# One way for h - tanh h instead of two: an expert kernel on one core, with a new order of its token stage

## Chip, core and metric

The kernel runs on one core of one Trainium2 chip. The metric is the device time in microseconds (us) of a run, as the median of several runs; lower is better. Everything is float32; large products split an operand into a rounded part and its remainder and use three matmuls.

## What is computed

Three layers, one behind the other (inputs are drawn at random; here cut to what matters):

```
X = rfft(x, axis=1)                       # x: 8 x 3072 x 256
Yr = Xr @ w_r - Xi @ w_i + b_r            # Yi alike; both shrunk by 0.01 towards 0
y = irfft(Y)                              # 24576 tokens x 256 from here on
h = y @ w_in                              # 2048 wide
x2 = (h - tanh(h)) @ w_out                # 256 wide
logits = x2 @ phi                         # 32 slots
d = softmax(logits, axis=0)               # over the 24576 tokens
slot_out = experts(d.T @ x2)              # 8 experts of 4 slots: relu(s @ w1[e]) @ w2[e]
out = softmax(logits, axis=1) @ slot_out
```

## The kernel before

The program has three stages. `spectral_phase` makes y by transforms in two factors, in 96 steps (8 batches of 12), and stores it in DRAM. Beside them it takes 32 pieces of the weights w_in and w_out through `load_w`, `narrow`, `use_w` and `fold_w`: a piece of w_in is split for the hidden layer (L457, L458), stored to `wi32`, turned by two transposes (L465) and multiplied into `wy` (L477); a piece of w_out is turned and multiplied with phi into `wp` (L487, L488). So `wp` is -w_out phi, and `wy` is w_in w_out phi.

`token_phase` works on 48 chunks of 512 tokens. h stands there with its 2048 rows in eight pairs of 128 (p = 0 to 7, four pairs of pairs w = 0 to 3). Chunk 0 is multiplied plainly (`plain`); from chunk 1 on `wino` uses a Winograd form: per w seven products P 1 to 7 of six matmuls each (L768), in three of six PSUM banks. ScalarE evicts P 1, 6, 7 and 4 into g (L779), VectorE adds what is in the other two banks (A, L786), ScalarE puts tanh over each finished g tile (G, L790, 1024 columns). So g holds tanh h. The logits take g with `wp` (L911) and, for the term in h, y itself with `wy` (L919, y loaded again by `load_raw`). For the dispatch d.T @ (h - tanh h), g is turned by VectorE's 32 x 32 transposes (T, L860), regrouped by DMAs from SBUF to SBUF (`reg`, L876) and multiplied with the turned softmax (D, L1042); y is turned too (L849), regrouped with g and multiplied (DY, L828), summed in `accy` (L836), and after the last chunk multiplied with w_in from `wi32` (L1213) and subtracted. The softmax over slots is divided here, in `combine_end` (L1019 to L1025), and stored in DRAM as `ctd`. For the tokens' own split into a rounded part and a remainder GpSimd subtracts (L666, L675, L681).

The order within a chunk is written out by hand: `PLAN` lists steps (name, which chunk relative to the present one, arguments), and `chunk(c)` issues them in that order. Every engine executes its own instructions in the order in which they were issued; so a step that waits holds up what stands behind it on its engine.

In the last chunk and after it, weights of the experts are loaded into tiles that come free (`weights`, `ew.load`, L1347, L1349, all from SyncE's queue), the last chunk is turned on TensorE (`turn_pe`, L889), and `expert_phase` multiplies slots, experts and, in 24 pairs of chunks, the output, which ScalarE and VectorE evict in halves (L1441, L1442).

```
            g = gs[c, p] if u else g_tile(c, p)
            nc.scalar.activation(g[:, u], o, AF.Tanh)
...
            nc.scalar.activation(wp[:, r, :], pw, AF.Copy, scale=-1.0)
...
            for name, d, *args in PLAN:
                k = c + d
```

## Time and profile before

| | |
|---|---|
| Median of 3 runs | 2144.37 us (2140.1 to 2145.66) |
| Profiled execution, first to last instruction (span) | 2137.1 us |
| Mean granted TensorE clock | 0.980 of full speed |
| TensorE matmuls busy | 2052.8 us, 96% of the span |
| VectorE busy | 1849.2 us, 87% |
| ScalarE busy | 1396.0 us, 65% |
| GpSimd busy | 642.6 us, 30% |
| Moved by DMA | 499.68 MB, 234 GB/s |

The profile is of one execution, and the only time that it has of its own is the span from its first to its last instruction; the median of the runs is 7.3 us longer, which is what lies around that span. In the profile PE is TensorE's matmuls, PEld its weight loads, DVE is VectorE, ACT ScalarE, POOL GpSimd, SP SyncE; SPq and ACTq are the DMA queues of SyncE and ScalarE. A matmul of float32 counts as two instructions, one of a rounded operand as one. A duration is that of one instruction from its start to its end; neighbours on TensorE overlap, so what one costs in a row is the distance of starts. "idle before" names what ended an engine's wait.

### The profile page before, as it was taken

To read this page: it belongs to the slowest core of one execution; us is meant where nothing else is said; L and a number is where in the kernel's file an instruction comes from. 1 tells how busy PE (TensorE), PEld (TensorE's weight loads), DVE (VectorE), ACT (ScalarE), POOL (GpSimd) and SP (SyncE) were. 2 spreads that over 40 slices of the span, in tenths; PEclk is the share of its full clock that TensorE was granted. 3 is DMA by queue.
4 is the path that set the end of the run, shared out by engine and by line. 5 is a ranking of instruction groups with operands and counts; after the bars stand their busy time and mean duration, and the time that the engine had idled before them with its cause. 6 is when DMAs were issued, how large, how long until landed. Compare 5 with 4: busy or idle time off the path is not lost.

```text
span 2137.1 us, 54258 instructions
## 1 busy us (share of the span) xinstructions
PE 2052.8 (96%) x21302; PEld 1732.6 (81%) x21302; DVE 1849.2 (87%) x3587; ACT 1396.0 (65%) x2309; POOL 642.6 (30%) x655
## 2 busy tenths in 40 slices
PE   5899999999999999999999999999999999999985
PEld 2678888887887888888888888888888888888743
DVE  3999888999995899999999999999999999999624
ACT  2456666666566777777777777777777777777614
POOL 0444444444443422222222222222222222222000
PEclk7999999999999999999999999999999999999986
DMA  9788999899657788888888888888888888888899
GB/s 273 225 242 267 284 283 286 269 283 293 202 198 205 194 208 213 207 213 209 207 203 209 208 208 210 219 204 208 209 206 208 209 206 210 214 209 208 254 401 388
DMA packets 260927, 499.68 MB, mean 234 GB/s; under 512 B 37312, under 2 KB 147648, under 8 KB 260416
## 3 DMA queue, kind: packets, MB, share of 16 engines
q1 hardware_dynamic: 259632, 494.60, 84.8%
q8 instruction: 169, 2.77, 0.6%
q10 hardware_dynamic: 1040, 1.61, 0.2%
q14 instruction: 86, 0.70, 0.1%
HBM read 166.28 MB, written 108.00 MB: 128 GB/s over the span
## 4 chain that ended last, share of the span: by engine, by line
PE 82%; DVE 8%; DMA 5%; ACT 2%; issue 1%; SPq 1%; POOL 0%; ACTq 0%; DVEq 0%; POOLq 0%
PE ph L768 44%; PE pl L911 8%; PE pd L1042 8%; PE pmix L328 4%; PE pi L413 4%; PE pf L287 3%; PE pi L385 3%; PE pa L328 3%; PE pf L251 2%; DVE sw L378 2%; DMA ewt<-in_moe_w 1%; DVE t L369 1%; DVE xml L299 1%; PE pl L828 1%; PE pl L919 1%
## 5 line engine op out<-in xcount | busy, mean ns | idle before, releaser
L779 ACT ACTIVATE g<-ph 128x512 f32<-128x512 f32 x752 | 448.6, 597 | 323.9 <-PE ph L768 285.8
L768 PE MATMUL ph<-th,s 128*128 128x256 f32 x2256 | 499.4, 288 | 3.3 <-ACT g L779 3.2
L860 DVE STREAM_TRANSPOSE gt<-g 128x512 f32<-128x512 f32 x752 | 472.0, 679 | 4.7 <-ACT g L742 4.0
L786 DVE TENSOR_TENSOR g<-ph,g 128x512 f32<-128x512 f32 x564 | 367.4, 672 | 85.3 <-ACT g L779 79.9
L790 ACT ACTIVATE g<-g 128x1024 f32<-128x1024 f32 x376 | 380.7, 1050 | 46.4 <-DVE g L786 46.4
L768 PEld LDWEIGHTS ph<-th,s 128*128 128x128 f32 x2256 | 383.7, 189 | 32.1 <-issue 19.4
L681 POOL TENSOR_TENSOR tl<-tr,th 128x512 fp32r<-128x512 f32 x94 | 121.5, 1293 | 949.4 <-ACT th L680 949.4
L768 PE MATMUL ph<-tl,s 128*128 128x256 f32 x1128 | 318.1, 282 | 0.0
L768 PE MATMUL ph<-yh,wl 128*128 128x256 f32 x1128 | 316.0, 280 | 0.0
L768 PE MATMUL ph<-y,wh 128*128 128x256 f32 x1128 | 315.4, 280 | 0.0
L768 PE MATMUL ph<-yh,wh 128*128 128x256 f32 x1128 | 315.1, 279 | 0.0
L378 POOL TENSOR_TENSOR sw<-t,c 64x256 f32<-64x256 f32 x192 | 169.7, 884 | 169.8 <-DVE c L370 130.9
L768 PEld LDWEIGHTS ph<-tl,s 128*128 128x128 f32 x1128 | 213.5, 189 | 0.0
L768 PEld LDWEIGHTS ph<-yh,wh 128*128 128x128 f32 x1128 | 213.0, 189 | 0.0
L768 PEld LDWEIGHTS ph<-y,wh 128*128 128x128 f32 x1128 | 212.3, 188 | 0.0
L768 PEld LDWEIGHTS ph<-yh,wl 128*128 128x128 f32 x1128 | 212.2, 188 | 0.0
L911 PE MATMUL pl<-g,wp 128*32 128x256 f32 x3072 | 193.2, 381 | 0.0
L1042 PE MATMUL pd<-gq,et 128*32 128x256 f32 x3008 | 172.7, 381 | 3.3 <-DMA gq<-gt 3.3
L1042 PEld LDWEIGHTS pd<-gq,et 128*32 128x32 f32 x3008 | 99.0, 111 | 68.1 <-issue 3.7
L287 PEld LDWEIGHTS pf<-f,a 128*128 128x128 f32 x768 | 102.0, 194 | 54.6 <-issue 37.8
L911 PEld LDWEIGHTS pl<-g,wp 128*32 128x32 f32 x3072 | 91.2, 110 | 56.4 <-issue 0.7
L413 PE MATMUL pi<-i,v 96*128 96x128 f32 x1024 | 134.5, 275 | 1.0 <-ACT yt L424 0.6
(216 smaller groups left out, 4279.4 us busy)
## 6 DMA issues: line engine op xcount, KB each, us to landing
gq<-gt SPq DMA_DIRECT2D x752, 160.0 KB, 3.5
gq<-gt SPq DMA_DIRECT2D x752, 128.0 KB, 3.2
xt<-in_x SPq DMA_DIRECT2D x64, 448.0 KB, 5.5
vd<-vs SPq DMA_DIRECT2D x96, 256.0 KB, 3.4
v<-vd SPq DMA_DIRECT2D x64, 384.0 KB, 5.3
yd<-yt SPq DMA_DIRECT2D x48, 512.0 KB, 5.7
y<-yd SPq DMA_DIRECT2D x48, 512.0 KB, 3.4
yr<-yd SPq DMA_DIRECT2D x48, 512.0 KB, 4.7
```

The lines of the kernel that those rows point to most:

```text
L287: nc.tensor.matmul(p[:, :, h, gg, :], t[:, gg, 128 * h:128 * h + 128], f2[:, 128 * g:128 * g + 128], start=True, stop=True,)
L328: nc.tensor.matmul(o, st[u], w[m], start=first and k == 0, stop=last and k == 2)
L378: eng.tensor_tensor(out=v[64 * ri:64 * ri + 64, gg], in0=t[q, e], in1=c[q, e], op=ALU.subtract)
L413: nc.tensor.matmul(p[:, a, :], t[:, 4 * u + a, :], i2[:, 96 * n2:96 * n2 + 128], start=True, stop=True)
L681: nc.gpsimd.tensor_tensor(out=lo, in0=t, in1=hi.bitcast(F32), op=ALU.subtract)
L768: nc.tensor.matmul(o[:, 256 * j:256 * j + 256], a[u][:, 128 * j:128 * j + 128], y[v], start=new and j == 0 and k == 0, stop=n in (2, 3, 4) ...
L779: nc.scalar.activation(e[n], o.rearrange("p (j n) -> p j n", j=2), AF.Copy)
L786: nc.vector.tensor_tensor(out=h, in0=o, in1=h, op=ALU.add)
L790: nc.scalar.activation(g, g, AF.Tanh)
L860: nc.vector.transpose(out=t[:, :, :, 2 * (p % 4) + u, :], in_=g[:, u, :].rearrange("p (q k i) -> p q k i", q=4, k=4))
L911: nc.tensor.matmul(lp[c][q:q + 32, 0:256], wp[:, 2 * p + f, :], half_of(c, gs[c, p + f // 2][:, f % 2], h), start=p == 0 and f < 2, stop=F ...
L1042: nc.tensor.matmul(o[32 * a:32 * a + 32, f], ex[c][:, k, :], g[a][:, k], start=k == 0, stop=k == 3)
```

## The change

g now holds h - tanh h itself. A finished quarter of two g tiles (512 columns, `quarter`) goes through tanh into one of four buffers `t0` to `t3` (G, `gate`), and GpSimd subtracts that from g (U, `ungate`); for P 4 the tanh is read from PSUM into g, without the eviction of before, and VectorE subtracts it from PSUM. All ways through y go: `load_raw`, `turn_yr`, `dy_mm`, `accum_y`, the logits with `wy`, the fold of w_in and `wi32`, and the product with w_in at the end; `wp` is now +w_out phi. The order is a new PLAN with U as a step. The division of the combine weights moves behind the output's matmuls, as a scale of its eviction in four pieces (`zt`); the sums are kept in `zs`. Output tiles lie in two PSUM tiles of half the size. In the last chunk each unit of G and U is issued as it gets ready, T and `reg` of the chunk before as soon as they can be, and eight loads (`early`) are issued from ScalarE's queue at set points.

```
-    ("G", -1, 6), ("P", 0, 0, 6), ("A", 0, 0, 2), ("T", -1, 7), ("loady", 1), ("splity", 1), ("L", -1, 0), ("DY", -2), ("L", -1, 2),
...
+    ("U", -1, 3, 3), ("U", -1, 3, 2), ("L", -1, 2), ("A", 0, 0, 2), ("U", -1, 3, 7), ("G", -1, 2, 3), ("D", -2), ("G", 0, 0, 2),
...
@@ use_w, fold_w
-                nc.sync.dma_start(out=wi32[128 * r:128 * r + 128, 256 * q:256 * q + 256], in_=t)
...
-            else:
-                nc.sync.dma_start(out=wo32.rearrange("(p F) m -> p F m", F=16)[:, r], in_=t)
+                return
+            nc.sync.dma_start(out=wo32.rearrange("(p F) m -> p F m", F=16)[:, r], in_=t)
...
+            if src is w_in:
+                return
...
-                    nc.tensor.matmul(pw, wt[:, k, :], wp[:, 2 * q + k, :], start=k == 0, stop=k == 1)
...
-            nc.scalar.activation(wp[:, r, :], pw, AF.Copy, scale=-1.0)
+            nc.scalar.activation(wp[:, r, :], pw, AF.Copy)
@@ token_phase
-        homes = chain(["g5"] + [f"g{k}" for k in range(5)], cycle([f"g{k}" for k in range(5)] + [f"x{k}" for k in range(4)] + ["x5"]))
+        homes = chain(
+            ("g5", "g0", "g1", "g2", "g3", "g4", "g0", "g1"),
+            cycle(("g2", "g5", "x0", "x2", "x3", "x5", "x1", "g0", "g1", "g3", "g4")),
+        )
...
             nc.scalar.activation(g[:, u], o, AF.Tanh)
+            nc.vector.tensor_tensor(out=g[:, u], in0=o, in1=g[:, u], op=ALU.subtract)
...
-            e = {1: ha and ha[:, :, 0:256], 6: ha and ha[:, :, 256:512], 7: hb and hb[:, :, 256:512], 4: hb and hb[:, :, 0:256]}
+            e = {1: ha and ha[:, :, 0:256], 6: ha and ha[:, :, 256:512], 7: hb and hb[:, :, 256:512]}
...
-        def gate(c, p):
-            g = gs[c, p]
-            nc.scalar.activation(g, g, AF.Tanh)
...
+        def gate(c, w, n):
+
+            g, o = quarter(c, w, n)
+            if n == 4:
+                nc.scalar.activation(g, o, AF.Tanh)
             else:
+                t = th[c, w, n] = ew.tyq.tile([128, 2, 256], F32, tag=f"t{next(units) % 4}", name="tanh")
+                nc.scalar.activation(t, g, AF.Tanh)
+
+        def ungate(c, w, n):
+
+            g, o = quarter(c, w, n)
+            if n == 4:
+                nc.vector.tensor_tensor(out=g, in0=o, in1=g, op=ALU.subtract)
             else:
+                eng = nc.vector if c == nch - 1 and sum(left) < 2 else nc.gpsimd
+                eng.tensor_tensor(out=g, in0=g, in1=th.pop((c, w, n)), op=ALU.subtract)
...
-            if p == 6:
-                for kk in range(2):
-                    for h in range(2):
-                        q = 64 * kk + 32 * h
-                        nc.tensor.matmul(
-                            lp[c][q:q + 32, 0:256], wy[:, kk], half_of(c, yr[c][:, kk], h), start=False, stop=True,
-                            skip_group_check=True,
-                        )
...
@@ combine_end
-            nc.vector.tensor_reduce(out=z, in_=lt, axis=AX.X, op=ALU.add)
-            nc.vector.tensor_scalar(out=z, in0=z, scalar1=1e-9, scalar2=None, op0=ALU.add)
-            nc.vector.reciprocal(out=z, in_=z)
-            nc.vector.tensor_tensor(out=lt, in0=lt, in1=z.to_broadcast([128, 4, 32]), op=ALU.mult)
+            nc.vector.tensor_reduce(out=ew.zs[:, c], in_=lt, axis=AX.X, op=ALU.add)
@@ chunk, for the last chunk
+                if name == "P":
+                    for w, n in held[:-1]:
+                        do("G", c, w, n)
+                        do("U", c, w, n)
+                    del held[:-1]
+                if name == "A" or name == "P" and args[1] == 4:
+                    held.append(args)
+                if name == "U" and d < 0:
+                    turn_rest(k)
+                if name in "PG":
+                    weights()
...
+        early = [
+            [2, [("D", last - 1)], (ew.load, 10, "h")],
+            [2, [("sum", last)] + [("T", last, p) for p in range(8)], (ew.load, 11, "x")],
+            [2, [("sum", last)] + [("T", last, p) for p in range(8)], (ew.load_ct, 0)],
+            [2, all_of(0), (ew.load, 0, "w0")],
+            [2, all_of(0) + all_of(1), (ew.load, 1, "s0", "s1")],
+            [2, all_of(1), (ew.load, 2, "w1")],
+            [2, all_of(1) + all_of(2), (ew.load, 3, "s1", "s2")],
+            [2, all_of(2), (ew.load, 4, "w2")],
+        ]
...
@@ after the last chunk
-                    nc.tensor.matmul(
-                        pu[32 * a:32 * a + 32, 128 * j:128 * j + 128], ew.aty[:, k, :], w[:, a],
...
-        nc.vector.tensor_tensor(out=acc, in0=acc, in1=pu, op=ALU.subtract)
@@ expert_phase
-            p = po.tile([128, 4, 2, 256], F32, tag="o", name="p_out")
+            p = [po.tile([128, 2, 2, 256], F32, tag=f"o{k}", name="p_out") for k in range(2)]
...
-                nc.scalar.activation(ot[:, 0:2, :], p[:, 0:2, j, :], AF.Copy)
-                nc.vector.tensor_copy(ot[:, 2:4, :], p[:, 2:4, j, :])
+                for a in range(4):
+                    if a < 2:
+                        nc.scalar.activation(ot[:, a], p[0][:, a, j], AF.Copy, scale=zt[:, a, i + j:i + j + 1])
+                    else:
+                        nc.vector.tensor_scalar(
+                            out=ot[:, a], in0=p[1][:, a - 2, j], scalar1=zt[:, a, i + j:i + j + 1], scalar2=None, op0=ALU.mult
+                        )
```

TensorE, in the middle of a token chunk, before: the logits of the chunk before (pl, L911 with g, L919 with y), the dispatch of the one before that (pd, L1042 with g; L828 with y), between hidden-layer matmuls (ph).

```order
L768 MATMUL ph<-th,s 128x256
L911 MATMUL pl<-g,wp 32x256 x8
L828 MATMUL pl<-gq,et 32x64 x16
L911 MATMUL pl<-g,wp 32x256 x8
L1042 MATMUL pd<-gq,et 32x256 x32
L911 MATMUL pl<-g,wp 32x256 x16
L919 MATMUL pl<-yr,wy 32x256 x4
L768 MATMUL ph<-th,s 128x256
```

The same place now:

```order
L763 MATMUL ph<-th,wl 128x256
L868 MATMUL pl<-g,wp 32x256 x16
L988 MATMUL pd<-gq,et 32x256 x32
L868 MATMUL pl<-g,wp 32x256 x16
L763 MATMUL ph<-th,s 128x256
```

The two products of y are gone; the logits with g and the dispatch stand in a row as before. (Here a float32 matmul is one row; the profile counts it twice.)

GpSimd, one token chunk in the middle, before: all that it does is the next chunk's split of y and of its sums (tr).

```order
L681 TENSOR_TENSOR tl<-tr,th 128x512 x2
L675 TENSOR_TENSOR tr<-y 128x256
L675 TENSOR_TENSOR tr<-y,tr 128x256
L675 TENSOR_TENSOR tr<-y 128x256
L675 TENSOR_TENSOR tr<-y,tr 128x256
L666 TENSOR_TENSOR y<-y,yh 128x1024
```

One token chunk now:

```order
L805 TENSOR_TENSOR g<-g,tanh 128x2x256 x8
L666 TENSOR_TENSOR tr<-y 128x256
L666 TENSOR_TENSOR tr<-y,tr 128x256
L666 TENSOR_TENSOR tr<-y 128x256
L666 TENSOR_TENSOR tr<-y,tr 128x256
L657 TENSOR_TENSOR y<-y,yh 128x1024
L805 TENSOR_TENSOR g<-g,tanh 128x2x256 x3
L672 TENSOR_TENSOR tl<-tr,th 128x512
L805 TENSOR_TENSOR g<-g,tanh 128x2x256
L672 TENSOR_TENSOR tl<-tr,th 128x512
```

Twelve subtractions (L805) stand between the operations of before, eight of them in a row.

ScalarE, in the last chunk, now (evictions L774, tanh L796 and, from PSUM, L793; the loads L1298, L1300, L1258 stood in SyncE's queue before, or were issued later):

```order
L1298 DMA gq<-in_moe_w 128x512 x4
L774 ACTIVATE g<-ph 128x2x256
L796 ACTIVATE tanh<-g 128x512 x2
L793 ACTIVATE g<-ph 128x2x256
L774 ACTIVATE g<-ph 128x2x256
L796 ACTIVATE tanh<-g 128x512
L888 ACTIVATE le<-pl 64x256
L774 ACTIVATE g<-ph 128x2x256
L1300 DMA ewt<-in_moe_w 128x512 x4
L796 ACTIVATE tanh<-g 128x512
L774 ACTIVATE g<-ph 128x2x256
L1298 DMA ewt<-in_moe_w 128x512 x4
```

After these come one load of combine weights (L1258), an eviction and eight more loads (L1300), 21 in all, before the last tanh's. In the old order ScalarE's queue has no DMA there.

## Rows read from the trace of the kernel before

**Rows 1.** Busy time by stretch; columns: stretch, length, engines busy (instructions), clock, DMA.
```profile
core 0: us, PE busy (x) PEld busy (x) DVE busy (x) ACT busy (x) POOL busy (x), PEclk, DMA share, GB/s
...
400.00:500.00 100.00, 98.88 (x742) 81.04 (x741) 93.46 (x182) 64.21 (x118) 45.60 (x54) 1.00 0.90 279
...
600.00:700.00 100.00, 94.55 (x670) 81.20 (x669) 73.81 (x135) 60.01 (x111) 41.38 (x43) 0.98 0.65 201
...
1500.00:2000.00 500.00, 500.00 (x5984) 437.38 (x5984) 459.35 (x905) 360.07 (x567) 134.94 (x120) 1.00 0.86 208
...
2050.00:2060.00 10.00, 9.74 (x100) 6.23 (x100) 0.71 (x4) 0.20 (x1) 0.00 (x0) 0.83 1.05 394
```

**Rows 2.** Chain of waits through one chunk: start us, us, engine, tile, line.
```profile
1952.72 1.00 PE pl L911 x16
1953.72 0.45 PE pl L828 x32
1954.17 0.86 PE pl L911 x16
1955.03 3.45 PE pd L1042 x64
1958.49 1.73 PE pl L911 x32
1960.21 0.43 PE pl L919 x8
1960.64 20.29 PE ph L768 x168
```

**Rows 3.** Timeline of TensorE, four successive steps of the spectral stage: start us, us.
```profile
432.42 1.02 PE L385 MATMUL pi<-sw,i 128*128 128x512 f32 x2
...
438.41 1.02 PE L385 MATMUL pi<-sw,i 128*128 128x512 f32 x2
...
444.70 1.02 PE L385 MATMUL pi<-sw,i 128*128 128x512 f32 x2
...
451.17 1.02 PE L385 MATMUL pi<-sw,i 128*128 128x512 f32 x2
```

**Rows 4.** Groups by line, TensorE, weight pieces: count, then busy us, mean ns.
```profile
L465 PE MATMUL pt<-ident,dl 128*128 128x128 f32 x64 | 14.0, 300 | 4.3 <-ACT xmf L296 3.9
...
L477 PE MATMUL pw<-wp,wt 128*128 128x32 f32 x64 | 10.0, 280 | 0.0
```

**Rows 5.** Groups by line, VectorE, ScalarE and GpSimd; after the bar idle before them.
```profile
L779 ACT ACTIVATE g<-ph 128x512 f32<-128x512 f32 x752 | 448.6, 597 | 323.9 <-PE ph L768 285.8 <-DVE gt L860 3.3 <-POOL wl L712 0.8
...
L790 ACT ACTIVATE g<-g 128x1024 f32<-128x1024 f32 x376 | 380.7, 1050 | 46.4 <-DVE g L786 46.4
...
L786 DVE TENSOR_TENSOR g<-ph,g 128x512 f32<-128x512 f32 x564 | 367.4, 672 | 85.3 <-ACT g L779 79.9 <-PE ph L768 1.1
...
L681 POOL TENSOR_TENSOR tl<-tr,th 128x512 fp32r<-128x512 f32 x94 | 121.5, 1293 | 949.4 <-ACT th L680 949.4
...
L1022 DVE TENSOR_TENSOR lt<-lt,cz 128x128 f32<-128x128 f32 x48 | 107.1, 2231 | 1.7
...
L849 DVE STREAM_TRANSPOSE gt<-yr 128x512 f32<-128x512 f32 x94 | 60.8, 684 | 0.0
...
L1010 DVE TENSOR_TENSOR lt<-lt,cm 128x128 f32<-128x128 f32 x48 | 15.1, 314 | 1.7
```

**Rows 6.** Timeline of GpSimd and of VectorE, one moment of a chunk.
```profile
1508.95 2.40 POOL L666 TENSOR_TENSOR y<-y,yh 128x1024 fp32r<-128x1024 f32 x1
...
1509.15 2.36 DVE L1022 TENSOR_TENSOR lt<-lt,cz 128x128 f32<-128x128 f32 x1
```

**Rows 7.** Timeline of TensorE behind the last chunk; in brackets idle time and releaser.
```profile
2012.98 3.54 PE L1042 MATMUL pd<-gq,et 128*32 128x256 f32 x32 [3.29 <-DMA gq<-gt]
...
2033.28 2.03 PE L1213 MATMUL ph<-ewt,aty 128*32 128x128 f32 x64 [0.25 <-DVE aty L1207]
```

**Rows 8.** Timeline of SyncE's DMA queue, weight loads after the last chunk.
```profile
2013.26 12.96 SPq L1349 DMA_DIRECT2D ewt<-in_moe_w  x20
```

**Rows 9.** Chain of waits, last link before the first output.
```profile
2064.03 8.75 DMA ect<-ctd
```

More of the change, by code (lines that the diff above doesn't have):

```diff
@@ L815, in token_phase @@
-        dy = {}
-        def dy_mm(c):
-            beside = c < nch - 1
-            o = dy[c] = lp[c + 1][:, 256:320] if beside else bank()[:, 0:64]
-            if beside:
-                y = [g[:, 0:256].rearrange("p (k f) -> p k f", k=4) for g in gq[c, 0]]
-            else:
-                y = [yq[c][:, a] for a in range(4)]
-            for k in range(4):
-                for a in (3, 2, 1, 0):
-                    nc.tensor.matmul(
-                        o[32 * a:32 * a + 32], ex[c][:, k, :], y[a][:, k], start=k == 0 and not beside, stop=k == 3,
-                        skip_group_check=True,
-                    )
@@ L1001, in combine @@
         def combine(c):
-            o = lr.pop(c)
+            o = lr[c]
             lt = sp.tile([128, 4, 32], F32, tag="lt", name="lt", bufs=1)
@@ new lines, in chunk, with turn_rest @@
+                if name == "A" or name == "P" and args[1] == 4:
[4 more added lines that the diff above has]
+                    weights()
+            for w, n in held:
+                do("G", c, w, n)
+                do("U", c, w, n)
+        def turn_rest(c):
+            for h in range(2):
+                ready = 0
+                for p in range(4 * h, 4 * h + 4):
+                    if all(("U", c, p // 2, n) in done for n in ((4, 7) if p % 2 else (2, 3))):
+                        do("T", c, p)
+                        ready += 1
+                if ready == 4:
+                    for part in ((0, 1), (2,))[h]:
+                        do("reg", c, part)
@@ new lines, in all_of @@
+        def all_of(w):
+            return [("P", nch - 1, w, n) for n in range(1, 8)]
+        last = nch - 2
+        early = [
[8 more added lines that the diff above has]
+        ]
@@ L1113, in token_phase, with weights @@
+        def weights(flush=False):
+            for e in list(early):
+                n, keys, (f, *args) = e
+                if all(k in done for k in keys) and (not flush or e is not None):
+                    e[0] -= 1
+                    if e[0] < 0 or flush:
+                        f(*args, eng=nc.scalar)
+                        early.remove(e)
         c = 0
@@ L1376, in expert_phase @@
         at, z = ew.at, ew.z
+        zs = ew.zs.rearrange("p c k o -> p (c k o)")
+        nc.vector.tensor_scalar(out=zs, in0=zs, scalar1=1e-9, scalar2=None, op0=ALU.add)
+        nc.vector.reciprocal(out=zs, in_=zs)
+        zt = ew.gp.tile([128, 4, nch], F32, tag="g4", name="zt")
+        for k in range(4):
+            for a in range(4):
+                nc.vector.tensor_copy(zt[32 * k:32 * k + 32, a], ew.zs[32 * a:32 * a + 32, :, k, 0])
         p_in = ps.tile([128, 256], F32, tag="a", name="p_in")
@@ L1474, in kernel_body @@
         ew.open_early()
[L1475 to L1476 removed]
+        spectral = spectral_phase(tc, nb, x, w_r, w_i, b_r, b_i, tb, yd, w_in, w_out, phi, ident, wo32, wh, wl, wp, ew)
+        token = token_phase(tc, nch, yd, wh, wl, wp, ident, ew)
         last = NG // 2 * nb
```

214 lines of the change are left out of this document (65 added, 149 removed), and 22 rows, old and new, of the table PLAN.

## Prediction

> **What bounds the kernel now.** I read the busy time by stretches first. In the long token stage TensorE is busy for all of its 500 us, VectorE for 459, ScalarE for 360, GpSimd for 135, at full clock; the DMA share is 0.86 [rows 1]. A busy TensorE need not be the bound, so I read next the chain of waits through one token chunk. It consists of TensorE alone: 168 matmuls of the hidden layer (20.29 us), the logits (1.00, 0.86 and 1.73 us), the dispatch (3.45 us) and two groups that this change removes, 0.45 and 0.43 us [rows 2]. They add up to 28.21 us with no wait between them, so a chunk costs what TensorE's instructions cost. 48 chunks make nearly two thirds of the span.
>
> In the spectral stage TensorE is busy 98.9 of 100 us and VectorE 93.5 [rows 1]; a second engine is close, so I looked for steps that differ in TensorE's work alone. The column transforms (L385) of four successive steps start at 432.42, 438.41, 444.70 and 451.17: steps of 5.99, 6.29 and 6.47 us [rows 3]. The second has the two transposes of a weight piece in it (L465), the third its fold (L477), the first neither. An addition to TensorE's queue lengthens the step by its own length: TensorE is the bound here too.
>
> At the end the DMA engines are full, at 394 GB/s [rows 1], and the first output waits for a load of the combine weights [rows 9].
>
> **The change, part by part.** *1. Token chunks.* Before, g held tanh h, so that both the logits and the dispatch needed a second way, through y: 8 instructions for logits (L919) and 32 for dispatch (L828). Both go; nothing is added on TensorE. Per chunk 0.43 + 0.45 = 0.88 us off 28.21 leaves 27.33. Over the 47 chunks that run in this manner that is 41.4 us, if TensorE stays the bound; this is the largest term.
>
> What the other engines then have to do in 27.33 us: busy times per chunk are those of the stretch over 500/28.21 = 17.7 chunks [rows 1].
> - GpSimd had 7.6 us. It gets 12 subtractions of 128x512 from SBUF. The nearest row is its subtraction of that size, 1.293 us [rows 5]: 15.5 us, together 23.1, or 85% of the period. It becomes a busy engine from an idle one.
> - VectorE had 25.9 us. It loses two transposes of y (2 x 0.684) and the division of the combine weights (2.231), and gets four subtractions from PSUM (0.672 each, the price of its additions) [rows 5]. That leaves 25.0, or 91%, against 92% before. Small operations that also go are not counted.
> - ScalarE had 20.3 us. It loses 4 evictions (0.597) and 8 tanh of 1024 columns (1.050), and gets 16 tanh of 512 columns at some 0.6 [rows 5]: 19.1 us, or 70%.
>
> So no engine passes TensorE by its sum. But a unit now goes a longer way: eviction, addition, tanh into one of four buffers, subtraction on GpSimd, and only then transposes and logits. In the new order, ScalarE's tanh of a unit waits until GpSimd has subtracted the fourth unit before it, and behind that tanh in ScalarE's queue stand evictions that free PSUM banks for TensorE. The bank of the h tiles whose tanh is read from PSUM is now kept until VectorE's subtraction. Bounds of this term: nothing below, since the order of before shows no idle TensorE with VectorE at 92%; above, half of what was gained, 20 us, because I can place no wait over 0.4 us per chunk. I take 3 us, near the lower end, since the row nearest to it is the chunk with no wait [rows 2].
>
> *2. Does GpSimd slow VectorE?* The division of before took 2.231 us on average, where a subtraction of the same shape took 0.314 [rows 5]. The timeline shows why: GpSimd's operation ran from 1508.95 for 2.40 us, so to 1511.35; the division began at 1509.15 and ended at 1511.51, just behind it [rows 6]. VectorE's additions with one operand in PSUM were not held up in such stretches: their mean is 0.672. Of VectorE's operations in the new chunk only the subtraction of the row maximum has two operands in SBUF; with GpSimd busy 85% of the time it waits half of 1.293 us, so 0.55 us, which brings VectorE to 93%. This is inside term 1.
>
> The Trainium skill speaks against putting work on GpSimd: Perfetto Trace Analysis, section Optimizing Scalar/DVE Operations, warns that the two engines share a read port, "so offloading operations between those two might not help". Its page SBUF — State Buffer, section Who interferes with whom, restricts this to VectorE instructions with two inputs in SBUF or in a two-port mode; by that page the sum stays as it is, 2094.5, by the wider warning it would be some 2400, the third rival below. This case's 2.231 against 0.314 us agrees with the narrower form.
>
> *3. Spectral stage.* For the 16 pieces of w_in the transposes, the fold, their evictions and a store go; w_out's 16 stay. Half of the 64 transposes and all 64 matmuls of that line go [rows 4]. By the steps, a piece costs 6.29 - 5.99 = 0.30 and 6.47 - 5.99 = 0.48 us: 16 x 0.78 = 12.5 us at most. VectorE's work per step stays nearly the same, 93.5% of 6.25 us (the mean of the three) = 5.8, and some steps are shorter than 6 us; late in the stage it may hold the step. If it holds a quarter of these steps, 9.4 us remain. I take 10.5.
>
> *4. Start of the token stage.* Chunk 0 gets 16 subtractions on VectorE, 16 x 0.672 = 10.8 us, in a stretch of 100 us in which it was busy 74 [rows 1]. GpSimd had 41 us there, most of it in the second half, where the subtractions of chunk 1 (15.5 us) now join. TensorE was already idle 5.5 us of it. Bounds: 0 and 8 us lost (half of the 15.5). I take 3.
>
> *5. The end.* Before, dispatch of the last chunk but one stood still for 3.29 us for its regrouped tiles, and 2.03 us of matmuls (L1213) plus their operand brought y's way back into the sum [rows 7]. The second goes, with some 2 us of other products of y: about 4 us. In the last chunk 21 weight loads are issued from ScalarE's queue. An issue took SyncE 12.96/20 = 0.65 us on a full queue [rows 8]: up to 13.7 us beside 19.1 of work in 27.33, so ScalarE may be late by 5 us there. In return these 5.5 MB no longer stand in the last 60 us, where 394 GB/s make 14 us of them and where the first output waited for a load [rows 9]; the chain of matmuls behind the last chunk then decides, and TensorE was busy for 9.7 of 10 us of the same stretch [rows 1], so little of the 14 comes out. The halves of PSUM and the scaling in four pieces hide under the output's DMA. Bounds: 12 us gained, 6 lost; I take 4 gained.
>
> Sum against the profiled span of 2137.1: -41.4 + 3 - 10.5 + 3 - 4 = -49.9. The median of the runs shown, 2144.37, stands 7.3 above that span; the launch around it is not touched. 2144.4 - 49.9 = **2094.5 us**.
>
> **Rivals.** *A new wait takes much of it back:* the four tanh buffers tie ScalarE to GpSimd, and TensorE waits for a bank in every chunk. For it: three engines above 85%, and a unit's way is longer by one engine. Against it: the sums leave 4 us of GpSimd and 2 of VectorE per chunk. At 0.4 to 0.8 us per chunk the gain shrinks by 19 to 38 us: 2107 to 2137, when the 3 us already counted are left in.
>
> *GpSimd becomes the bound, and the kernel is slower:* this decides from (28.21 - 7.6)/12 = 1.72 us per subtraction. At 1.9 us a chunk takes 7.6 + 22.8 = 30.4 us, 3.1 more than forecast: 2094.5 + 47 x 3.1 = 2240. For it: its instructions are the slowest per column of all, and VectorE hardly pauses. Against it: 1.293 us was measured with VectorE as busy as that.
>
> *The port holds up all of VectorE:* if the 16 additions and subtractions with one operand in PSUM waited as the division did, 16 x 0.55 = 8.8 us would put VectorE at 34 us and the kernel at some 2400. The 0.672 us of its additions speak against it. It gets 0.02.
>
> *The saving is hidden anyway,* since VectorE's dependences set the pace: within 0.3% of 2144. The unbroken chain of TensorE speaks against it.
>
> **How the numbers follow.** The forecast, TensorE still the bound, gets 0.70 with 2080 to 2107: its sum with the bounds of terms 3 to 5. The first rival gets 0.18; hidden anyway 0.05; GpSimd as the bound 0.05; the port 0.02. About 0.3% (6.4 us) is what a measurement of this kernel can tell from no change. Faster: 0.70 + 0.18 = 0.88; same 0.05; slower 0.07. The range takes the forecast's with 2 us below it, and the nearer two thirds of the first rival's: 2078 to 2126.
>
> **What would show it.** Right: a chain through a chunk of matmuls alone with a period of 27.3 us, no rows for the ways through y, GpSimd busy 80 to 87% in the token stage with subtractions of 1.3 us, spectral steps of 6.0 us where there were 6.29 and 6.47. Wrong: idle TensorE before hidden-layer matmuls, put down to ScalarE's evictions (first rival); subtractions over 1.6 us (second); VectorE's additions well above 0.67 us (third); a last chunk far longer than the others, or a first output that waits for a load as long as before (term 5).

## The result, and the profile after

The change took the kernel from 2142.23 us (median of 4 runs) to 2113.64 us (2110.15 to 2114.07, 4 runs): a ratio of 0.9868, 95% interval 0.9849 to 0.9888. The profiled spans are 2137.1 and 2111.8 us, so the pair of traces has to account for 25.3 us. The forecast was 2094.5 in 2078 to 2126: the time moved as forecast and lies inside the range, 19 us off. The parts show three terms off by 10 to 30 us, in ways that partly cancel.

To place the 25.3 us I use four marks that both timelines have: the last column transform of the spectral stage; the first hidden-layer matmul of chunk 1; the same of chunk 47 (47 chunks x 168 = 7896 such matmuls, so each 168th begins a chunk); the end. The dispatch makes a bad mark: the new order puts more hidden-layer groups in front of it.

| Stretch | before | after | change | forecast |
|---|---|---|---|---|
| to the last column transform (640.73, 640.28) | 640.7 | 640.3 | -0.5 | -10.5 |
| from there to chunk 1 (678.65, 679.60) | 37.9 | 39.3 | +1.4 | +3, with the next row |
| 46 chunks (to 1977.88, 1927.48) | 1299.2 | 1247.9 | -51.3 | -37.5 |
| last chunk and everything behind it | 159.2 | 184.3 | +25.1 | -4.9 |

In the third row the other 43 chunks ran at 27.05 us, before at 28.21. The first three took 84.9 us (679.60 to 764.47), 3.7 more than three of 27.05; before they took 86.0, 1.3 more than three of 28.21. So some 2.4 us were lost there, to the start.

The busy time by stretches, columns as in [rows 1], of the kernel after:

```profile
core 0: us, PE busy (x) PEld busy (x) DVE busy (x) ACT busy (x) POOL busy (x), PEclk, DMA share, GB/s
400.00:500.00 100.00, 98.22 (x717) 78.91 (x717) 93.93 (x178) 60.70 (x114) 45.81 (x55) 1.00 0.90 271
600.00:700.00 100.00, 91.10 (x622) 78.89 (x621) 74.73 (x133) 56.29 (x107) 38.38 (x40) 0.95 0.54 171
...
1500.00:1900.00 400.00, 400.00 (x4394) 353.18 (x4393) 367.93 (x725) 275.23 (x530) 340.19 (x282) 1.00 0.75 179
...
1970.00:1980.00 10.00, 1.93 (x16) 0.59 (x16) 6.37 (x16) 5.94 (x12) 3.73 (x3) 0.50 0.88 226
1980.00:1990.00 10.00, 3.74 (x32) 2.05 (x32) 3.59 (x10) 0.31 (x1) 0.00 (x0) 0.50 0.96 269
```

In the token stage GpSimd went from 27% to 85% busy, VectorE stayed at 92%, ScalarE fell from 72% to 69%, and TensorE is still busy throughout. The chain through one chunk, answering to [rows 2], is still TensorE alone:

```profile
1509.00 20.00 PE ph L763 x168
1529.01 1.86 PE pl L868 x32
1530.87 3.45 PE pd L988 x64
1534.32 1.73 PE pl L868 x32
1536.05 20.00 PE ph L763 x168
```

Both ways through y are gone, and the period is 27.05 us (1509.00 to 1536.05), 0.28 less than forecast: the 168 hidden-layer matmuls take 20.00 where they took 20.29. Most of this is a small wait that the chain of before does not show. Once in each chunk a weight load of TensorE waited 0.18 us for an eviction by ScalarE; the row is for 750 to 1925 us of the kernel before (us in total, times, longest):

```profile
PEld ph L768 <- ACT g L779: 7.4, 42, 0.2
```

The kernel after has no such row. Costliest groups, columns as in [rows 5]:

```profile
L805 POOL TENSOR_TENSOR g<-g,tanh 128x512 f32<-128x512 f32 x560 | 711.1, 1296 | 169.5 <-ACT tanh L796 169.5
L784 DVE TENSOR_TENSOR g<-ph,g 128x512 f32<-128x512 f32 x564 | 372.8, 681 | 66.5 <-ACT g L774 36.1 <-PE ph L763 20.4 <-ACT tanh L796 0.7
L796 ACT ACTIVATE tanh<-g 128x512 f32<-128x512 f32 x564 | 336.9, 622 | 112.4 <-DVE g L784 83.1 <-POOL g L805 18.3 <-DMA ewt<-in_moe_w 11.0
...
L959 DVE TENSOR_TENSOR lt<-lt,cm 128x128 f32<-128x128 f32 x48 | 28.3, 589 | 1.7
```

GpSimd's subtraction costs 1.296 us (1.293 was taken), VectorE's additions with an operand in PSUM 0.681 (0.672 before) beside a GpSimd that is busy 85% of the time, and the row maximum's subtraction, both operands in SBUF, 0.589 (0.314 before). By the Trainium skill (SBUF — State Buffer, section Who interferes with whom) VectorE operations with at most one operand in SBUF, outside the two-port modes, do not contend with GpSimd, and those with two do. This trace agrees: only the last of the three grew clearly.

In the spectral stage the column transforms, answering to [rows 3], and the chain of waits of about the same stretch:

```profile
435.46 1.12 PE L387 MATMUL pi<-sw,i 128*128 128x512 f32 x2
441.58 1.02 PE L387 MATMUL pi<-sw,i 128*128 128x512 f32 x2
447.91 1.12 PE L387 MATMUL pi<-sw,i 128*128 128x512 f32 x2 [0.17 <-POOL sw L380]
454.71 1.13 PE L387 MATMUL pi<-sw,i 128*128 128x512 f32 x2 [0.54 <-POOL sw L380]
460.50 1.02 PE L387 MATMUL pi<-sw,i 128*128 128x512 f32 x2
```

Steps of 6.12, 6.33, 6.80 and 5.79 us stand where 5.99, 6.29 and 6.47 stood, with less work on TensorE, which now waits. In the chain of 440 to 470 us every share was TensorE's before; now it is the DMA of one raw weight piece until 443.1 and then VectorE alone (sw, t, xml and others) until 469.5, with pauses below 1 us.

The end is where the forecast broke. Timelines of the kernel after: TensorE's rows with idle time in front (in brackets, with its releaser), then SyncE's and ScalarE's DMA queues with ScalarE's first operation behind its loads, then SyncE's waits from 1936 to 2000 (us in total, times, longest):

```profile
1973.26 1.93 PE L868 MATMUL pl<-g,wp 128*32 128x256 f32 x16 [9.87 <-POOL g L805]
1982.04 3.74 PE L988 MATMUL pd<-gq,et 128*32 128x256 f32 x32 [6.85 <-DVE acc L996]
1993.10 3.76 PE L988 MATMUL pd<-gq,et 128*32 128x256 f32 x32 [7.32 <-DMA gq<-gt]
```
```profile
1940.53 20.89 SPq L833 DMA_DIRECT2D gq<-gt  x16
...
1964.12 23.36 SPq L833 DMA_DIRECT2D gq<-gt  x16
```
```profile
1960.90 10.23 ACTq L1300 DMA_DIRECT2D ewt<-in_moe_w  x8
1971.23 1.67 ACT L796 ACTIVATE tanh<-g 128x512 f32<-128x512 f32 x3 [10.98 <-DMA ewt<-in_moe_w]
```
```profile
SPq L833 <- DMA ewt<-in_moe_w: 20.1, 7, 8.6
```

Eight issues hold ScalarE for 10.23 us while tanh waits behind them. The 32 regrouping issues (L833), on which the dispatch of chunk 46 waits, take 20.89 + 23.36 us; and SyncE waits 20.1 us in them for loads of expert weights, which give the regrouping no data. Between 1970 and 1990 TensorE ran 5.7 of 20 us, at a granted clock of 0.50, its lower level. From the last hidden-layer matmul to the first output it took 83.6 us (1963.1 to 2046.7), before 65.3 (2006.2 to 2071.5).

Why SyncE waits for ScalarE's loads is written in the program. This is its list of SyncE's DMA instructions with the semaphores that each waits on, four rows of an ordinary chunk, four of the last:

```
2022 L833 DMA gq_27044<-gt_26819 32x1024 [waits DMAHW0_49]
2023 L833 DMA gq_27044<-gt_26819 32x1024 [waits DMAHW1_49]
2024 L833 DMA gq_27044<-gt_26819 32x1024 [waits DMAHW2_49]
2025 L833 DMA gq_27049<-gt_26819 32x1024 [waits DMAHW3_49]
...
2080 L833 DMA gq_27618<-gt_27537 32x1024 [waits DMAHW2_49]
2081 L833 DMA gq_27618<-gt_27537 32x1024 [waits DMAHW5_49]
2082 L833 DMA gq_27618<-gt_27537 32x1024 [waits DMAHW0_49]
2083 L833 DMA gq_27623<-gt_27537 32x1024 [waits DMAHW1_49,PE_49]
```

Eight completion semaphores (DMAHW0 to 7) are dealt out in turn to the transfers of both queues, and each transfer waits for the one before it on its semaphore. In the ordinary chunk the numbers follow one another; in the last some are missing: ScalarE's loads have them. So the two queues, which look independent, wait for each other.

### The profile page after: what moved, and what is told of

Its sections match the earlier page's. It is cut to its first block, busy times and chain, and to the rows that moved or that the text cites. A ratio compares the mean times of both kernels' runs of the same rounds, so it can differ in the third digit from the quotient of the medians.

```text
span 2111.8 us, 51281 instructions
## 1 busy us (share of the span) xinstructions
PE 1991.0 (94%) x19214; PEld 1689.9 (80%) x19214; DVE 1817.2 (86%) x3555; ACT 1313.2 (62%) x2527; POOL 1347.8 (64%) x1215
## 4 chain that ended last, share of the span: by engine, by line
PE 75%; DVE 13%; DMA 6%; issue 2%; ACT 1%; SPq 1%; POOL 1%; ACTq 0%; DVEq 0%; POOLq 0%
PE ph L763 43%; PE pl L868 8%; PE pd L988 8%; PE pmix L330 3%; PE pi L415 3%; DVE sw L380 3%; PE pf L289 2%; PE pi L387 2%; PE pa L330 2%; PE pf L253 2%; DVE t L371 2%; DVE xml L301 1%; DVE t L360 1%; DMA out_dram<-gq 1%; DMA raw<-in_moe_w_in 1%
## 5 line engine op out<-in xcount | busy, mean ns | idle before, releaser
L805 POOL TENSOR_TENSOR g<-g,tanh 128x512 f32<-128x512 f32 x560 | 711.1, 1296 | 169.5 <-ACT tanh L796 169.5
L774 ACT ACTIVATE g<-ph 128x512 f32<-128x512 f32 x564 | 333.2, 591 | 243.0 <-PE ph L763 231.4
L817 DVE STREAM_TRANSPOSE gt<-g 128x512 f32<-128x512 f32 x752 | 479.2, 680 | 2.3 <-DMA gq<-gt 1.8
L763 PE MATMUL ph<-th,s 128*128 128x256 f32 x2256 | 456.2, 285 | 8.6 <-ACT g L774 4.9
L784 DVE TENSOR_TENSOR g<-ph,g 128x512 f32<-128x512 f32 x564 | 372.8, 681 | 66.5 <-ACT g L774 36.1
L796 ACT ACTIVATE tanh<-g 128x512 f32<-128x512 f32 x564 | 336.9, 622 | 112.4 <-DVE g L784 83.1
L763 PEld LDWEIGHTS ph<-th,s 128*128 128x128 f32 x2256 | 369.8, 191 | 28.7 <-issue 19.3
L320 POOL TENSOR_TENSOR xml<-xmf,xmh 128x256 fp32r<-128x256 f32 x96 | 74.4, 775 | 204.3 <-issue 144.1
L868 PE MATMUL pl<-g,wp 128*32 128x256 f32 x3072 | 185.6, 382 | 9.9 <-POOL g L805 9.9
```

Source lines behind the costliest of these rows:

```text
L320: nc.gpsimd.tensor_tensor(out=lo[:, 0], in0=sm, in1=hi[:, 0].bitcast(F32), op=ALU.subtract)
L763: nc.tensor.matmul(o[:, 256 * j:256 * j + 256], a[u][:, 128 * j:128 * j + 128], y[v], start=new and j == 0 and k == 0, stop=n in (2, 3, 4) ...
L774: nc.scalar.activation(e[n], o.rearrange("p (j n) -> p j n", j=2), AF.Copy)
L784: nc.vector.tensor_tensor(out=h, in0=o, in1=h, op=ALU.add)
L796: nc.scalar.activation(t, g, AF.Tanh)
L805: eng.tensor_tensor(out=g, in0=g, in1=th.pop((c, w, n)), op=ALU.subtract)
```

## The experiments

Twelve kernels were run; the figures to compare with are those of the kernel after: span 2111.8, ratio 0.9868, 184.3 us from the start of the last chunk to the end.

**e1_sync_queue: the early loads from SyncE.**
```
-                        f(*args, eng=nc.scalar)
+                        f(*args, eng=nc.sync)
```


> The early weight loads of the last chunk are issued by SyncE instead of ScalarE; nothing else changes. Theory A (ScalarE stands still behind its own load issues: 10.98 us before its tanh at 1971.23): its idle time of 10.98 us goes, the tail of chunk 46 (second half of its dispatch, 1993.1 in the changed kernel) comes 6 to 10 us earlier, span 2102 to 2106 against 2111.8. Rival B (the DMA engines are full and the regrouping of g is behind the loads, whoever issues them): the second half of dispatch of chunk 46 starts at 1990 or later, span 2109 to 2118.

Measured: ratio 0.9751 (0.9721 to 0.9781), span 2089.9, 163.5 us from the last chunk's start (1926.3). The dispatch of chunk 46 runs in one piece from 1967.93.

```profile
1940.01 10.04 SPq L833 DMA_DIRECT2D gq<-gt  x16
...
1950.78 11.09 SPq L833 DMA_DIRECT2D gq<-gt  x16
1961.90 2.01 SPq L1298 DMA_DIRECT2D gq<-in_moe_w  x4
```

Rival B falls, and theory A was too small: I had named only ScalarE's idle time. In one queue the loads stand behind the regrouping, and the regrouping is back at 0.63 to 0.69 us per issue. The run cures both ills at once, so it can't tell their shares.

**e2_loads_after: the early loads held until the regrouping is issued, from SyncE.**
```
-                if name in "PG":
-                    weights()
...
-                        f(*args, eng=nc.scalar)
+                        f(*args, eng=nc.sync)
```


> The early loads are held back until all regrouping transfers of g are issued, and then issued by SyncE. Theory B (loads in the way of the regrouping: 32 issues took 20.89 + 23.36 us where they took about 0.65 us each in the steady state): 32 regrouping issues in some 21 us together, second half of dispatch of chunk 46 at 1973 to 1978 instead of 1993.1, first output at 2028 to 2036 instead of 2046.7, span 2093 to 2101. Rival C (the loads are needed early, so that the first expert layer or the first output then waits for them): the dispatch comes earlier all the same, but TensorE waits for loads behind it, first output at 2042 or later, span 2107 or more.

Measured: ratio 0.9749 (0.9729 to 0.9768), span 2083.6, 156.6 us from the last chunk's start (1927.0): 27.7 us less than in the kernel after and 2.6 less than before. The regrouping took 10.90 + 11.18 us, the dispatch of chunk 46 started at 1963.59, the first output at 2018.32. Theory B holds, by more than expected. In SyncE's queue and TensorE's:

```profile
1938.23 10.90 SPq L833 DMA_DIRECT2D gq<-gt  x16
...
1949.87 11.18 SPq L833 DMA_DIRECT2D gq<-gt  x16
```
```profile
1963.59 5.03 PE L988 MATMUL pd<-gq,et 128*32 128x256 f32 x64 [6.19 <-DMA gq<-in_moe_w]
```

The profile puts the 6.19 us down to a load; e1 and e10 have the same wait (6.20 us) and put it down to VectorE's sum (acc), so it isn't the load's doing. Behind it one wait for a load is left, 3.40 us for wo.

**e10_hold_scalar: held as in e2, but issued by ScalarE.**
```
-                if name in "PG":
-                    weights()
```


> The early loads are held back as in the run that issues them behind the regrouping, but ScalarE issues them. Theory I (what cost most in the changed kernel were the regrouping transfers, slowed from 0.65 to 1.3 us each by loads beside them): the second half of the dispatch of chunk 46 comes nearly as early as with SyncE, 1966 to 1975, span 2083 to 2092. Rival J (ScalarE's queue, standing behind its issues, costs most): its evictions for the last chunk are late by 8 to 13 us, and the span is 2093 to 2105.

Measured: span 2117.4, worse than the kernel after, and outside both expectations.

```profile
1949.18 45.15 SPq L833 DMA_DIRECT2D gq<-gt  x16
```
```profile
1968.42 23.40 ACTq L1298 DMA_DIRECT2D ewt<-in_moe_w  x20
```
```profile
1999.94 3.97 PE L988 MATMUL pd<-gq,et 128*32 128x256 f32 x32 [31.55 <-DMA gq<-gt]
```
```profile
SPq L833 <- DMA gq<-in_moe_w: 17.5, 2, 16.6
```

The second of sixteen regrouping issues waited 16.6 us for a load that ScalarE had not even issued yet (its first left at 1962.25, behind the last tanh): the DMA engines were all but idle meanwhile (share 0.07 from 1950 to 1960), so it was not bandwidth. The program of e10 shows the reason: that issue waits on DMAHW5, which was dealt to one of ScalarE's loads before it. Theory I, which blamed traffic, falls, and rival J's price was too low by the same mechanism. e10 and e2 differ in the issuing engine alone: some 34 us of span.

**e12_gpsimd_queue: the early loads at their old places, from GpSimd, whose transfers have semaphores of their own.**
```
-                        f(*args, eng=nc.scalar)
+                        f(*args, eng=nc.gpsimd)
```


> The early loads stand at the places where the changed kernel has them, so beside the regrouping, but GpSimd issues them. Transfers issued by SyncE and ScalarE share eight completion semaphores in turn, and each waits for the transfer before it on its semaphore; those of GpSimd have semaphores of their own. Theory N (the regrouping is late because its issues wait on semaphores for loads of the other queue: SyncE waited 20.1 us for loads, 7 times, which give it no data): SyncE's waits for loads at the regrouping's line fall below 3 us, 16 issues take 10 to 12 us, the second half of the dispatch of chunk 46 starts at 1966 to 1978 instead of 1993.1. Rival O (the DMA engines are shared by loads and regrouping, whatever the queue): 16 issues still take 18 us or more, dispatch at 1985 or later.

Measured: span 2104.3. SyncE no longer waits for any load at L833, and its sixteen issues take 10.18 and 14.81 us, with the loads moving beside them:

```profile
1937.49 10.18 SPq L833 DMA_DIRECT2D gq<-gt  x16
...
1948.67 14.81 SPq L833 DMA_DIRECT2D gq<-gt  x16
```
```profile
1973.38 3.72 POOL L805 TENSOR_TENSOR g<-g,tanh 128x512 f32<-128x512 f32 x3
```

For the regrouping theory N is right, with a mild share for rival O (14.81 against some 11 us). The dispatch of chunk 46 started no earlier all the same (1981.37 against 1982.04, though now in one piece), since GpSimd's own subtractions stand behind its loads: from 1956 to 1973 it issued loads and nothing else. A queue on an engine with other work is paid by that work. The Trainium skill (Trainium Kernel Development and Optimization, section Key Constraints) says that issuing from several engines "only saves the sequencer's issue time". e12 agrees as far as it goes: beside the loads sixteen regrouping issues took 14.81 us, in e1's single queue 11.09. e10 shows that a second queue can also cost time.

**e3_zt_behind: the scales' reciprocal and sixteen small copies behind the relu, nothing else.** The block from `zs = ` to the loop over `zt` moves from in front of `p_in` to in front of `p_o`.

> The sixteen small copies of the scales and their reciprocal (L1330 to L1334) are issued behind the relu of the expert layer instead of in front of its first product; the loads stay as in the changed kernel. Theory (they stand in the chain, TensorE waits 4.05 us for the copy behind them): first output 3.5 to 4.5 us earlier, at 2042 to 2043, span 2107 to 2108.5. Rival (without them the same product waits for its weights): less than 1.5 us.

Measured: span 2104.8; from the last dispatch to the first output 32.7 us (2007.06 to 2039.73), where the kernel after took 38.5 (2008.25 to 2046.71): 5.8 us, more than the 3.5 to 4.5 that the copies were expected to give. The product p_h, in the kernel after and here:

```profile
2020.84 6.44 PE L1311 MATMUL p_h<-ewt,s 128*32 128x512 f32 x40 [4.05 <-DVE s L1345]
```
```profile
2015.99 4.50 PE L1311 MATMUL p_h<-ewt,s 128*32 128x512 f32 x40 [0.39 <-DVE s L1337]
```

Besides 3.66 us of waiting, the same 40 matmuls ran 1.94 us faster: behind the wait TensorE's granted clock was 0.50 from 2020.8 to 2024, without it 1.00. Here a wait on the chain cost more than its length.

**b1_after_zt: e2 and e3 together.**

> Loads behind the regrouping on SyncE's queue and the copies of the scales behind the relu, both together. If the two gains add, span 2083.6 - 5 = 2077 to 2080, and about 0.972 of the kernel before. Rival P (behind the regrouping the loads now bound the tail at 390 to 400 GB/s, so that the first product waits for weights in place of the copies): span 2082 to 2085, 0.975.

Measured: ratio 0.9744 (0.9730 to 0.9759), span 2084.0: no better than e2 alone (0.9749). Rival P: the wait at p_h is as short in e2 (0.39 us), since there the copies ran while TensorE waited for wo anyway. The gains of e2 and e3 don't add. In b1's profile the tail is even longer, 160.5 us against 156.6 in e2, and 2.9 of this is one product: the 40 matmuls of p_h took 7.37 us with the granted clock at 0.50 until 1997, in e2 4.50 at 1.00, behind the same wait of 0.39 us. In b1 the clock fell at 1986.8, behind idle times of 1.73 and 0.58 us; so it can be low there without a long wait just before.

**e9_before_no_y: the kernel before, without the chunks' matmuls of y.**
```
-                        start=p == 0 and f < 2, stop=False, skip_group_check=True,
+                        start=p == 0 and f < 2, stop=p == 6 and f >= 2, skip_group_check=True,
...
-            if p == 6:
+            if False:
...
+            if beside:
+                return
             o = dy[c] = lp[c + 1][:, 256:320] if beside else bank()[:, 0:64]
```


> The kernel before, with its own order, but without the logits' and the dispatch's matmuls of y in the chunks (0.43 and 0.45 us; the last chunk keeps its own); everything else stays, the transposes of y on VectorE and the division too. The product through y is left out of the output. Theory F (the removed matmuls are the whole of the gain, 0.88 us, and the remaining 0.29 us of the 1.165 comes from the new order, in which no hidden-layer matmul waits for its bank): a chunk takes 27.3 to 27.4 us. Rival G (VectorE at 92% already holds the old order, so that removing TensorE's work alone does not come out): 27.6 to 28.2 us. Rival H (the order makes no difference): 27.05.

The edit also leaves out VectorE's sum of these products in the chunks (`accum_y`, 0.274 us each; not printed above).

Measured: the dispatches start 27.99 us apart (median over the chunks), 0.22 less than 28.21. Rival G. Busy time from 1000 to 1500 us, the wait of TensorE's weight loads from 750 to 1925, and the chain of 1500 to 1560:

```profile
1000.00:1500.00 500.00, 488.61 (x5260) 430.20 (x5260) 461.41 (x894) 364.08 (x573) 138.07 (x122) 1.00 0.88 211
```
```profile
PEld ph L768 <- DVE g L786: 34.7, 43, 0.8
```
```profile
by line: DVE gt L864 25.2%; PE ph L768 17.5%; DVE g L786 15.7%; SPq L880 14.9%; DMA gq<-gt 4.6%; DVE lt L1026 4.5%; DVE cz L1024 4.4%; issue 4.1%; DVE gt L853 2.0%; DVE le L948 1.4%; DVE m L963 1.1%; ACT g L779 1.0%; DVE nm L970 0.7%; DVE n
```

With 0.88 us taken off TensorE it is idle 11.4 of 500 us: in every chunk a weight load waits some 0.8 us for VectorE's addition. More than half of the chain is VectorE's, with steps of the division (cz, lt) that took 2.4 us beside a GpSimd operation of 2.4. So in the order of before VectorE was at most 0.22 us behind TensorE, and most of the gain needed something besides TensorE's saving: the work that the change took off VectorE (the division, the transposes of y) or its new order. These two weren't tried apart.

**e11_more_gpsimd: two more subtractions on GpSimd in each chunk.**
```
+                if n == 2 and w in EXTRA and c < nch - 1:
+                    nc.gpsimd.tensor_tensor(out=t, in0=g, in1=t, op=ALU.subtract)
```
with `EXTRA = (0, 2)`.

> GpSimd makes two more subtractions of 128x512 in each chunk (of units that are already done, into a tanh buffer that is no longer needed): 2 x 1.296 us on top of 22.9, so 25.5 of 27.05 us, 94%. The buffers come free 1.3 us later in two of four rounds. Theory K (GpSimd has the slack that the sums say, 4.1 us in a chunk, and the four tanh buffers are enough): the period stays 27.05 to 27.1. Rival L (the buffers tie ScalarE to GpSimd, the first rival of the prediction, and only just not in the changed kernel): TensorE waits in every chunk, period 27.3 us or more.

Measured: the median period stays 27.05 us with GpSimd busy 94%:

```profile
1000.00:1500.00 500.00, 500.00 (x5453) 444.81 (x5446) 469.64 (x903) 344.60 (x663) 469.71 (x388) 1.00 0.75 179
```

Theory K: the slack is there, and the prediction's first rival would have needed more than 2.6 us of further work. The span grew to 2118.7 all the same. Of these 7.0 us the first three chunks took 3.8: chunk 2 took 33.4 us (from hidden-layer matmul to hidden-layer matmul, 710.57 to 743.93) where the kernel after has 29.0. Another 2.7 came in the spectral stage, which the edit does not touch. The steady state has slack; the start has none.

**e5_less_vector: the last two of nine conversions of each w_in piece left out.**
```
+            if pieces[j][0] is w_in:
+                return
             scalar(hi, hi, 0x7FF00000, ALU.bitwise_and)
             both(l, hi, float(897 << 20), l, ALU.is_ge, ALU.mult)
```


> The last two of the nine conversions of each w_in piece on VectorE are left out, some 1.1 us of VectorE for each of 16 pieces (0.503 and 0.633 us); TensorE's instructions are the same. Theory D (in the stretch of the w_in pieces VectorE, held up by GpSimd, now sets the step): steps fall to TensorE's 5.7 to 6.1 us and the last column transform of the spectral stage starts 7 to 14 us earlier, at 626 to 633 instead of 640.3. Rival E (TensorE or the loads of the pieces set the step): less than 3 us, 637 or later.

Measured: last column transform at 630.6, span 2101.9. The eight profiles with an untouched spectral stage (the kernel after and seven runs) lie at 636.3 to 643.0, mean 639.2, so this is 5.7 us below the lowest and 8.7 below the mean. A better measure leaves out what comes before the pieces of w_in: from the 47th step's column transform, with which they begin, to the last one of the stage. These are its ends in the kernel before, then in the kernel after:

```profile
338.25 1.02 PE L385 MATMUL pi<-sw,i 128*128 128x512 f32 x2
...
640.73 0.38 PE L385 MATMUL pi<-sw,i 128*128 128x256 f32 x1
```
```profile
336.49 1.02 PE L387 MATMUL pi<-sw,i 128*128 128x512 f32 x2
...
640.28 0.38 PE L387 MATMUL pi<-sw,i 128*128 128x256 f32 x1
```

| Kernel | from the 47th step's column transform to the last, us |
|---|---|
| before; e9 | 302.5; 304.1 |
| the eight | 300.6 to 304.7, mean 302.5 |
| e5 | 295.5 |

There e5 is 5.2 us below the lowest and 7.0 below the mean. Theory D fits. But the two conversions are also the last readers of the piece's raw buffer, of which there is one, so the next piece can be fetched earlier; the run doesn't separate VectorE's time from that round trip.

**b3_one_less: b1, with one conversion of each piece saved.**
```
-            scalar(lo, lo, 8, ALU.logical_shift_right)
...
-            both(l, lo, 2.0 ** -44, l, ALU.mult, ALU.mult)
+            both(l, lo.bitcast(mybir.dt.uint32), 2.0 ** -52, l, ALU.mult, ALU.mult)
```


> As b1_after_zt, with one of the nine conversions of every piece of w_in and w_out on VectorE saved for good: the low word is read as an unsigned integer and scaled by 2^-52, where before it was shifted right by 8 (0.503 us) and scaled by 2^-44. Theory D (VectorE sets the step in the stretch of the w_in pieces, and e5_less_vector took 1.14 us per piece off it for 8 to 10 us): 16 x 0.503 = 8 us less of VectorE there, 3 to 5 us of time, last column transform at 633 to 636 (the profiles of kernels with the same spectral stage lie at 636.3 to 643.0, mean 639.2), ratio 0.972 to 0.973 of the kernel before against 0.9744. Rival E (TensorE or the loads of the pieces): 637 or later, ratio 0.974 or more.

Measured: ratio 0.9732 (0.9719 to 0.9746), median 2083.09, last column transform at 635.4. The lowest of all by its median, but its interval overlaps that of b1, whose own profile stands at 636.3. From the 47th step's column transform to the last it took 301.6 us, 0.9 below the mean of the eight and inside their spread; 3 to 5 were expected, and its earlier end came ahead of that stretch. So theory D gets no clear support from it, though it took as much as 8 us off VectorE there.

**s1_shrink_scalar and b2_shrink_moved: the clamp from VectorE to ScalarE, two tries.** In s1 the two relu stand where the clamp stood and the subtractions move to the next step; in b2 (b1 with it) relu and subtractions are both in the next step.
```
-            nc.vector.tensor_scalar(out=c, in0=t, scalar1=LAM, scalar2=-LAM, op0=ALU.min, op1=ALU.max)
+            nc.scalar.activation(c, t, AF.Relu, bias=lam)
+            nc.scalar.activation(t, t, AF.Relu, bias=lam, scale=-1.0)
```


> In the spectral stage VectorE's clamp of each step (L372, 0.427 us) is replaced by two ScalarE operations of 128x512 (relu of t - lambda and of -t - lambda, about 0.6 us each), and the four subtractions move to the start of the next step. ScalarE goes from 61% to some 80%. Theory D (VectorE sets the step in the stretch of the w_in pieces): with 0.43 us less per step the stage ends 5 to 10 us earlier, last column transform at 630 to 635 instead of 640.3. Rival M (ScalarE, now later with its evictions, sets the step instead): 638 or later.

> As the run before it, and the clamp of the spectral stage is made by two ScalarE operations again, but at the start of the next step, when VectorE's sum has long been written, so that ScalarE no longer waits for it (266.9 us in the first try); the four subtractions follow in the same step. Theory D (VectorE sets the step in the stretch of the w_in pieces): last column transform at 629 to 636 instead of 640, span 4 to 10 us less than the run before it. Rival Q (the longer way through ScalarE, or the later subtractions, delay the column transforms): 641 or later.

Measured: spans 2313.9 and 2354.0; the last column transform at 842.2 and 906.1. In s1 ScalarE waits for VectorE's sum in every step, with the evictions behind it; in b2 TensorE waits for GpSimd's subtraction:

```profile
L376 ACT ACTIVATE c<-t,lam 128x512 f32<-128x512 f32 x96 | 69.3, 722 | 266.9 <-DVE t L375 266.9
```
```profile
L399 PE MATMUL pi<-sw,i 128*128 128x512 f32 x176 | 121.7, 780 | 180.4 <-POOL sw L392 180.4
```

Rivals M and Q, far beyond their stated size. The two say nothing on theory D: they moved a link between engines that wait for each other in every step, and I had counted its busy time alone.

## Why the prediction was right or wrong

**1. Token chunk (forecast -38.4 with its waits): right in mechanism, too small.** TensorE alone is the chain, as forecast, and the two groups are gone. The steps that failed are "with no wait between them" and the bound "nothing below": a wait of 0.18 us in each chunk was hidden in the row of hidden-layer matmuls, and it went. Instead of 3 us of new waits there are none, and the hidden-layer matmuls became 0.29 us shorter, so 1.16 us came off a chunk instead of 0.88. Whether the new order or the lighter VectorE removed the wait wasn't tried apart. Also unseen in the sum: "a chunk costs what TensorE's instructions cost" held for the kernel before with at most 0.22 us to spare (e9). A chain of one engine says who is late now, not who is next.

**2. GpSimd and the port: right in kind.** 1.296, 0.681 and 0.589 us; the rivals of a bound GpSimd and of a port that holds all of VectorE are refuted, the first with over 2.6 us to spare (e11). The wait of the row maximum's subtraction was put too high: 0.275 us, half of the 0.55 estimated.

**3. Spectral stage (forecast -10.5, at least 9.4): wrong.** The step that failed is "if it holds a quarter of these steps". TensorE's additions went, as said, but the pair of profiles shows 0.5 us. In the stretch of the w_in pieces two profiles of before took 302.5 and 304.1 us, the eight after 302.5 on average: 0.8 us, inside the spread of 4. What was taken off TensorE came back as waits, behind VectorE in the chain of 440 to 470 us. Whether VectorE's own time sets the pace or the fetch of the one raw buffer with it stays open: e5 shortens both, and b3 settles nothing. Zero should have been inside the bounds, as for every saving on an engine with a second one at 93%.

**4. Start of the token stage (forecast +3): right.** 1.4 us to the first hidden-layer matmul and 2.4 in the first three chunks, 3.8 together.

**5. The end (forecast -4, between -12 and +6): wrong in sign and size, +25.1 with the last chunk.** The step that failed is "ScalarE may be late by 5 us". The price of an issue, 0.65 us, came from one queue that waited at most 0.3 us at a time for its own loads; the eight in front of ScalarE's held tanh took 1.28 us each. Two queues that share semaphores wait for each other, and the regrouping, on which the dispatch of chunk 46 hangs, was not in the sum at all. The prediction's own sign of being wrong came true: the hidden-layer matmuls of the last chunk took 35.6 us, before 28.4. That the loads in themselves were no loss is shown by e2: behind the regrouping and in its queue, the same transfers leave a tail of 156.6 us, 2.6 shorter than before where 4.9 were forecast. How much of the loss was ScalarE standing still and how much the late regrouping isn't told apart: e1 and e2 cure both.

By spans the gain is 24.6 us short of the sum (-25.3 against -49.9): 30.0 in the last row of the table and 10.0 in the first, less 13.8 in the third and 1.6 in the second. By the median it is 19 short. The difference is in the base: I put 7.3 us around the span, but the profiled execution after took 2113.57 us with a span of 2111.8, so 1.8; the rest was the spread between executions.

That the time lies in the range is in part luck. Without the 13.8 us that the 46 chunks gave beyond the forecast it would have been some 2127, just outside. And 2113.6 is not in the 2080 to 2107 that the prediction gave to its own mechanism, which was right, but in the band of its first rival, whose new wait in every chunk is not in the trace. The bands were also added up loosely: with the bounds of terms 3 to 5 the forecast reaches 2110.6, and 19 to 38 us less of gain make 2113.5 to 2132.5, not 2107 to 2137.

## What to carry to other kernels

Before moving a transfer to another engine's queue, list what it shares with the old one: here eight completion semaphores, so that a queue in a hurry waited for one that was late, and an engine whose evictions or subtractions stood behind the issues; one queue in the right order beat two. When a saving is on an engine with a neighbour above 90%, put zero into its bounds, and test the neighbour by removing the saved work alone. Keep small operations for later use out of the chain's last links: in the kernel after, TensorE's granted clock was 0.50 behind a wait of 4 us there, which made the product behind it longer too.

## What was not expected of the hardware

- A transfer's issue can wait for a transfer of another queue that is not yet issued: 16.6 us with the DMA engines at a share of 0.07 (e10).
- Behind 4.05 us of idle time TensorE's granted clock was 0.50 from 2020.8 to 2024 us in the kernel after, and 40 matmuls took 6.44 us; in e3 they took 4.50.
- GpSimd at 94% beside VectorE at 94% cost the steady state nothing (e11).
- The end of the spectral stage moves by 6.7 us between profiles of kernels that are the same up to there (636.3 to 643.0). Some 3.5 us of this are there by the column transform of the 47th step (334.8 to 338.3), 4 come behind it. VectorE's wait for raw weight pieces between 330 and 560 us was 5.3 us in the kernel after and 1.4 in b1, but 2.8 in e2 and 3.2 in e12, which ended 2.8 us apart; the cause stays open.
